# Where ScalarE's read-outs of dense sums and the tanh stand between the exponentials of an attention block with an MLP beside it

## The chip, the cores and the metric

The kernel runs on one core of a Trainium2 chip. The metric is the device time of one execution in microseconds (us), lower is better. Three engines carry the work: TensorE (PE) multiplies, VectorE (DVE) takes row maxima, ScalarE (ACT) takes exponentials; GpSimd (POOL) does elementwise work on the side, and the DMA queue of SyncE (SP) moves data.

## The reference: what is computed

```python
xn = _layernorm(x, axis=-1)                        # x: 2048 x 512
qkv = (xn @ wqkv) ...                              # 32 heads of 16
p = _softmax(q k^T * 16 ** -0.5)                   # 2048 x 2048 for each head
A = (p v) @ wo
h = _gelu(xn @ w1 + b1)                            # 2048 x 1792, tanh form
B = h @ w2 + b2
return x + A + B
```

## The kernel before: how the work is tiled and ordered

**Units and halves.** The attention is cut into tasks of 4 heads by 512 queries, and each task into 16 units; there are 512 units, and `unit` (L633) writes out one of them. A unit has two halves. A half first issues a burst on TensorE: a block of scores S for a later unit, a block of transposed scores T, again an S and a T (`s_half` L245, `e_half` L291). VectorE reduces each S to row maxima (L257). ScalarE turns each T into exponentials `pe` (L302). Behind the burst come, side by side in the two row halves of the array, the products of exponentials and values into `pV` (`v_half` L305) and some *dense* products into `pD` (`dense` L575). A matmul of 64 rows uses one row half, so S beside T and V beside D run at once. V and the dense products change row halves by turns: in the first half of a unit (a = 0, called a B half below) V has rows 64 to 127 and the dense products rows 0 to 63; in the second (a = 1, an A half) it is the other way round. So the order is B, A, B, A and so on.

**Dense groups.** The dense work is everything else: projections of q and k (24 groups), the hidden layer of the MLP (56 groups, `hidden` L1042), its second matrix (16 groups, `store` L1066), the output projection (`finish` L1098). A `Group` (L411) is a list of products that sum into one bank of PSUM. A half issues `pace` products of one row half: FAST is 4, SLOW is 3, and MEAN alternates. Hidden groups alternate SLOW and FAST and so last 8 and 6 halves. A group's last product falls in an A half; the next group starts in the B half that follows.

**Read-outs.** When a group is complete, `ended` (L560) calls `end` (L444): ScalarE reads the sum out of PSUM (`pf` L502, `hh` L1045, `yt` L1068, `ys` L1109), and the bank goes back on a list. `unit` calls `ended` at the end of each half, so the read-out is issued ahead of the next burst's exponentials. `v_end` (L318) reads out `pV` in the same place at the end of each task (`osb` L328, always in a B half).

**GELU.** After `hh` a timed queue (`later` L211, `tick` L233, once a unit) hands out the GELU: three steps on POOL, then the tanh on ScalarE (`t` L1014), then four steps on POOL. `tick` stands behind `ended`, at the end of an A half: a tanh that falls due where a group ends is issued straight behind the read-out.

**Banks.** PSUM has eight banks in lists (L102): S and V share four, T and D the other four. `e_half` takes the bank at the head of list T and puts it at the tail. A dense group takes one bank off the head of the list with its first product (`hold` L112) and puts it at the tail in `end`. So three banks turn among the T blocks while a group holds the fourth, and a T block can start when the reader of its bank is done.

The order on each engine is as written; nothing is rescheduled.

Of the kernel before, what the change touches and what calls it, by code (L numbers as in the profile page):

```python
# [47 lines left out]
def layer_kernel(ctx: ExitStack, tc: tile.TileContext, x, wqkv, wo, w1, b1, w2, b2, out):  # L48
# [110 lines left out]
    def given(engine, ns):  # L159
        backlog[engine] += ns  # L160
# [17 lines left out]
    def leave(user, goes_on):  # L178

        p = newest.pop(user, None)  # L180
        if p is not None and goes_on:
            p.then_inc(turns, 1)
            tc.no_tile_sem_insts.add(p.ins.name)
            counted[0] += 1
            left.append(p)

    def enter():

        if left:
            goal[0] = f"turn{counted[0]}"  # L190
            for p in left:
                tc.add_to_no_dep_group(goal[0], p.ins)
            left.clear()
# [9 lines left out]
    def fetch_scale(m):  # L203

        scale_of[m] = nc.scalar.alloc_register(f"sexp{m}")
        nc.scalar.reg_load(scale_of[m], sexp[0:1, m:m + 1].bitcast(I32))

    mt_of, ptiles, pv_of, stores = {}, {}, {}, {}
    queue, slot = [], [0]

    def later(n, fn, local=False):  # L211
        queue.append((slot[0] + n, fn, local))

    def run_due():
        due = sorted((q for q in queue if q[0] <= slot[0]), key=lambda q: q[0])
        queue[:] = [q for q in queue if q[0] > slot[0]]
        for q in due:
            q[1]()


    steps, room = [], [0]

    def pooled(*todo):
        steps.extend(todo)

    def run_steps(all_of_them=False):
        room[0] = min(room[0], 0) + POOL_NS
        while steps and (room[0] > 0 or all_of_them):
            ns, fn = steps.pop(0)
            room[0] -= ns  # L230
            fn()

    def tick():  # L233
        run_due()
        run_steps()
        slot[0] += 1

    def flush():

        while steps or any(q[2] for q in queue):  # L240
            run_due()
            run_steps(True)
            slot[0] += 1

    def s_half(u, n):  # L245

        t, i = divmod(u, 16)
        g, qb = divmod(t, NQB)
        qt, kb = divmod(i, 4) if t else (i % 4, i // 4)
        if t not in mt_of:  # L250
            mt_of[t] = work.tile([P, 4, 4, 4], F32, name="mt", bufs=2)
        ks, qs = kst[g % 2], qst[g % 2]
        p, a = divmod(n, 2)
        r = slice(64 * a, 64 * a + 62)
        s = banks("S")
        tiled(None, s, qs[p][qb][r, qt * P:(qt + 1) * P], ks[p][kb][r, :], True, True)
        nc.vector.reduce_max(mt_of[t][:, n, qt, kb:kb + 1], s, axis=AX.X)  # L257
        given("dve", 600)
# [32 lines left out]
    def e_half(u, n):  # L291

        p, a = divmod(n, 2)
        t, kt = divmod(u, 16)
        g, qb = divmod(t, NQB)
        st = banks("T")
        r = slice(64 * a, 64 * a + 64)
        k0 = (kt % 4) * P
        tiled(None, st, kst[g % 2][p][kt // 4][r, k0:k0 + P], qst[g % 2][p][qb][r, :], True, True)
        pe = work.tile([P, QB], F32, name="pe", bufs=12)  # L300
        ptiles[u, n] = pe
        nc.scalar.activation(pe, st, AF.Exp, scale=scale_of[g // 2])  # L302
        given("act", 520)

    def v_half(u, a):  # L305

        t, kt = divmod(u, 16)
        g, qb = divmod(t, NQB)
        if kt == 0 and a == 0:
            pv_of[t] = hold("V", "S")  # L310
        pv = pv_of[t][0]
        r = slice(64 * a, 64 * a + 64)
        for h in (2, 3, 0, 1):
            c = (4 * g + h) * VW
            product("V", pv[32 * h:32 * h + 32, :], vv[r, kt, c:c + 32], ptiles[u, h][r],
                    start=(kt == 0 and a == 0), stop=(kt == 15 and a == 1))
# [240 lines left out]
                cur[0], spent[0] = None, True  # L557
        return cur[0]

    def ended():  # L560

        if cur[0] is not None and cur[0].over():
            done, cur[0] = cur[0], None
            done.end()

    def burst(gen, n):

        while n > 0 and (f := group(gen)) is not None:
            if not f.usable():
                break  # L570
            f.product(2)
            n -= 1
            ended()

    def dense(gen, side):  # L575

        f = group(gen)
        for _ in range(0 if f is None else f.pace[pos[0] % 2]):
            if not f.usable(side):
                return  # L580
            f.product(side)
# [25 lines left out]
    def spare(gen, side):  # L607

        if extra[0] is None and not spent[0]:
            f = next(gen, 0)  # L610
            spent[0] = f == 0
            extra[0] = Halves(f) if f else None
        if extra[0] is not None:
            extra[0].product(side)
            if extra[0].at == extra[0].n:
                extra[0] = None

    def land():

        while extra[0] is not None:  # L620
            for side in range(2):
                if extra[0] is not None:
                    spare(None, side)
        if cur[0] is not None:
            enter()
        for side in range(2):
            while cur[0] is not None and cur[0].left(side):
                nc.tensor.drain()
                while cur[0].left(side):
                    cur[0].product(side)  # L630
        ended()

    def unit(gen):  # L633


        u = pos[0]
        e = u - LEAD
        if e >= 0 and e % (2 * NQB * 16) == 0 and e < NU:
            fetch_scale(e // (2 * NQB * 16))
        if u == LEAD and cur[0] is not None:  # L640
            burst(gen, cur[0].left())
        pos[0] += 1
        for a in range(2):
            for b in range(2 * a, 2 * a + 2):
                if u < NU:
                    s_half(u, b)
                elif u > NU:
                    spare(gen, b % 2)
                if 0 <= e < NU:
                    e_half(e, b ^ 1)  # L650
            if u < LEAD:
                burst(gen, LFILL[u - 16] // 2)
            if e >= 0:
                enter()

                w, r = (e - 2, 1) if a == 0 else (e - 1, 0)
                live = 0 <= w < NU
                new = r == 0 and w % 16 == 0
                if live and not new:
                    v_half(w, r)  # L660
                dense(gen, 1 - r)
                if live and new:
                    v_half(w, r)

                for user, goes_on in (("V", live and not (r == 1 and w % 16 == 15)),
                                      ("D", cur[0] is not None and not cur[0].over())):
                    leave(user, goes_on)
                for k in backlog:
                    backlog[k] = max(0, backlog[k] - HALF)
                if live and r == 1:  # L670
                    v_end(w)
                ended()

            if a == 0 and u % 16 == 0 and u // 16 - 1 in stores:
                stores.pop(u // 16 - 1)()
        if u < NU:
            s_end(u)
        tick()
# [325 lines left out]
    def mlp():  # L1004
# [3 lines left out]
        done = set()  # L1008

        def gelu(hh, g, b, f):  # L1010
            t1 = m2.tile([P, QB], F32, name="t1", bufs=2)

            def tanh():
                nc.scalar.activation(t1, t1, AF.Tanh, scale=GELU_C * GELU_A)  # L1014
                given("act", 600)
                later(1, rest, True)

            def rest():
                pooled((690, lambda: nc.gpsimd.tensor_scalar(t1, t1, 1.0, gs[:, 1:2], op0=ALU.add, op1=ALU.mult)),
                       (1280, lambda: nc.gpsimd.tensor_tensor(t1, t1, hh, op=ALU.mult)),  # L1020
                       (620, lambda: nc.gpsimd.tensor_scalar(g[:, 0, f, :], t1, 1.0, 0.0, op0=ALU.mult, op1=ALU.add)),
                       (1160, lambda: nc.gpsimd.tensor_tensor(g[:, 1, f, :], t1, g[:, 0, f, :], op=ALU.subtract)),  # L1022
                       (0, lambda: done.add((b, f))))

            pooled((1040, lambda: nc.gpsimd.tensor_tensor(t1, hh, hh, op=ALU.mult)),  # L1025
                   (620, lambda: nc.gpsimd.tensor_scalar(t1, t1, 1.0, 1.0 / GELU_A, op0=ALU.mult, op1=ALU.add)),
                   (1280, lambda: nc.gpsimd.tensor_tensor(t1, t1, hh, op=ALU.mult)),  # L1027
                   (0, lambda: later(2, tanh, True)))

        for b in range(NQB):  # L1030
            xb = xbs[b]
# [114 lines left out]
    with ExitStack() as st3:  # L1146
# [46 lines left out]
        while pos[0] < NU + LEAD + 2:  # L1193
            more_stacks()
            unit(fil)
# [32 lines left out]
```

## Time and profile before

| what | us |
|---|---|
| median of 3 runs (1520.38 to 1526.5) | 1525.09 |
| the profiled execution, its own time | 1520.55 |
| its span in the trace | 1518.8 |
| TensorE busy | 1489.5 |
| VectorE busy | 1402.2 |
| ScalarE busy | 1245.6 |
| GpSimd busy | 664.5 |

The span begins with the first instruction and ends with the last; 1.75 us of the execution lie around it. A group of instructions is shown as line, engine, operation, output<-inputs, shapes, count, then busy time and mean duration, then the idle time ahead of it and what ended it. Ends of matmuls are modelled, so a busy TensorE says little about whether it could do more. A view of the instructions in order of time merges neighbours of one kind ("x4"), its first column is the start, its second the length.

### The profile page before, as it was taken

The page shows a single profiled execution, that of the slowest core. Times are in us where ns is not written, and L with a number is a line of the kernel's source. Part 1 is how long each engine was busy: PE and PEld are TensorE (multiplying, and loading weights), DVE is VectorE, ACT ScalarE, POOL GpSimd, SP SyncE. Part 2 cuts the span into 40 slices and gives each one's busy share as a digit, 9 for nine tenths or more (in the row PEclk, how much of TensorE's full clock was granted, in tenths as well). Part 3 has the DMA queues.
Part 4 walks back from the last instruction along what each step waited for, and adds up shares of the span by engine and source line. Part 5 has one row for each costly group of instructions (what it writes and reads, how often), then busy time and mean ns, then how long its engine had stood idle before and what let it go on. Part 6 is the DMA issues. An engine that isn't in the chain of part 4 may idle for free.

```text
span 1518.8 us, 86848 instructions
## 1 busy us (share of the span) xinstructions
PE 1489.5 (98%) x39407; PEld 815.9 (54%) x39407; DVE 1402.2 (92%) x2367; ACT 1245.6 (82%) x2318; POOL 664.5 (44%) x686
## 2 busy tenths in 40 slices
PE   8999999999999999999999999999999999999998
PEld 3434555555555555555555555555555555555553
DVE  7899989999999999999999999999999999999933
ACT  5327778899988888898888898988888898888884
POOL 4113597547771112777411167751116775211110
PEclk9999999999999999999999999999999999999998
DMA  6454567542122201121011211122101201121422
GB/s 208 127 155 158 166 219 211 180 126 77 58 69 66 61 26 42 36 84 50 23 49 41 66 42 40 36 78 63 34 25 56 77 27 29 50 60 50 136 65 95
DMA packets 113674, 123.76 MB, mean 81 GB/s; under 512 B 24988, under 2 KB 85276, under 8 KB 113304
## 3 DMA queue, kind: packets, MB, share of 16 engines
q1 hardware_dynamic: 113304, 118.21, 25.4%
q8 instruction: 308, 5.05, 1.4%
q14 instruction: 62, 0.51, 0.1%
HBM read 80.61 MB, written 37.34 MB: 78 GB/s over the span
## 4 chain that ended last, share of the span: by engine, by line
PE 79%; DVE 16%; issue 2%; ACT 2%; DMA 1%; POOL 0%; SPq 0%; POOLq 0%
PE pV L169 23%; PE pD L169 19%; PE pT L169 17%; PE pS L169 16%; DVE mt L257 13%; PE pT L435 1%; PE pD L435 1%; DVE amx L709 1%; ACT pe L302 1%; ACT t L1014 1%; PE pT L528 1%; PE pV L528 0%; DMA m_d<-mhl 0%; DMA xs<-in_A_x_dram 0%; DMA wch<-in_B_w_dram 0%
## 5 line engine op out<-in xcount | busy, mean ns | idle before, releaser
L257 DVE TENSOR_REDUCE mt<-pS 128x1 f32<-128x512 f32 x2048 | 1304.5, 684 | 52.5 <-PE pS L169 34.8
L302 ACT ACTIVATE pe<-pT 128x512 f32<-128x512 f32 x2048 | 1100.8, 599 | 162.9 <-PE pS L169 78.6
L169 PE MATMUL pV<-pe,vv 64*32 64x512 f32 x8192 | 1076.3, 595 | 0.1
L169 PE MATMUL pT<-qst,kst 64*32 64x512 f16 x8192 | 718.3, 378 | 8.8 <-ACT pe L302 7.9
L169 PE MATMUL pS<-kst,qst 62*32 62x512 f16 x8192 | 624.3, 378 | 5.2 <-DVE mt L257 3.6
L169 PEld LDWEIGHTS <-kst 64*32 64x32 f16 x8192 | 285.7, 91 | 203.9 <-issue 103.6
L169 PEld LDWEIGHTS <-qst 62*32 62x32 f16 x8192 | 273.3, 92 | 206.3 <-issue 58.2
L169 PE MATMUL pD<-w_s,g 64*32 64x512 f16 x5376 | 364.6, 376 | 0.0
L169 PE MATMUL pD<-xb,wc 64*32 64x512 f16 x5376 | 360.9, 377 | 0.0
L169 PEld LDWEIGHTS pV<-pe,vv 64*32 64x32 f32 x8192 | 181.0, 105 | 88.3 <-PE pV L169 4.3
L1070 POOL TENSOR_TENSOR xa<-xa,yt 128x512 f32<-128x512 f32 x16 | 20.5, 1282 | 319.0 <-ACT yt L1068 319.0
L169 PEld LDWEIGHTS <-wc 64*32 64x32 f16 x5376 | 116.9, 91 | 41.6
L169 PEld LDWEIGHTS <-g 64*32 64x32 f16 x5376 | 112.2, 91 | 45.3
L169 PE MATMUL pD<-xt,wqk_h 64*32 64x512 f16 x2016 | 134.7, 377 | 1.7 <-issue 1.5
L1025 POOL TENSOR_TENSOR t<-hh 128x512 f32<-128x512 f32 x56 | 58.3, 1041 | 132.7 <-ACT hh L1045 121.8
L358 POOL TENSOR_TENSOR osb<-osb,rb 128x512 f32<-128x512 f32 x31 | 39.9, 1287 | 135.1 <-DMA rb<-den_d 76.0
L1027 POOL TENSOR_TENSOR t<-t,hh 128x512 f32<-128x512 f32 x56 | 71.9, 1284 | 4.7
L1020 POOL TENSOR_TENSOR t<-t,hh 128x512 f32<-128x512 f32 x56 | 71.8, 1281 | 4.7
L1022 POOL TENSOR_TENSOR g<-t,g 128x512 f16<-128x512 f32 x56 | 65.2, 1165 | 4.7
L169 PEld LDWEIGHTS <-wqk_h 64*32 64x32 f16 x2016 | 47.5, 92 | 23.4 <-issue 6.2
L169 PE MATMUL pD<-wo_s,oc 64*32 64x512 f16 x828 | 54.5, 378 | 0.0
L1045 ACT ACTIVATE hh<-pD,b_s,fac 128x512 f32<-128x512 f32 x56 | 43.6, 779 | 9.4 <-PE pT L169 3.3
(141 smaller groups left out, 862.4 us busy)
## 6 DMA issues: line engine op xcount, KB each, us to landing
wch<-in_B_w_dram SPq DMA_DIRECT2D x28, 512.0 KB
wc<-w_d SPq DMA_DIRECT2D x56, 256.0 KB
qk_d<-stg SPq DMA_DIRECT2D x32, 256.0 KB
rb<-den_d SPq DMA_DIRECT2D x124, 64.0 KB
w_d<-wsp SPq DMA_DIRECT2D x28, 256.0 KB
kst<-qk_d SPq DMA_DIRECT2D x128, 48.0 KB
qst<-qk_d SPq DMA_DIRECT2D x128, 48.0 KB
xs<-in_A_x_dram SPq DMA_DIRECT2D x16, 256.0 KB
```

The lines of the kernel that those rows point to most:

```text
L169: p = nc.tensor.matmul(*args, **kw)
L257: nc.vector.reduce_max(mt_of[t][:, n, qt, kb:kb + 1], s, axis=AX.X)
L302: nc.scalar.activation(pe, st, AF.Exp, scale=scale_of[g // 2])
L358: pooled((1280, lambda: nc.gpsimd.tensor_tensor(osb, osb, rb, op=ALU.mult)), (620, lambda: nc.gpsimd.tensor_scalar(ot[:, 0], osb, 1.0, 0.0 ...
L435: nc.tensor.matmul(self.bank, lhs, rhs, start=start, stop=self.last and self.over())
L528: nc.tensor.matmul(pj, xt[:, i, c, t * P:(t + 1) * P], wh[j][:, c, :], start=(n == 0), stop=(n == 11))
L1020: (1280, lambda: nc.gpsimd.tensor_tensor(t1, t1, hh, op=ALU.mult)),
L1022: (1160, lambda: nc.gpsimd.tensor_tensor(g[:, 1, f, :], t1, g[:, 0, f, :], op=ALU.subtract)),
L1025: pooled((1040, lambda: nc.gpsimd.tensor_tensor(t1, hh, hh, op=ALU.mult)), (620, lambda: nc.gpsimd.tensor_scalar(t1, t1, 1.0, 1.0 / GELU_A ...
L1027: (1280, lambda: nc.gpsimd.tensor_tensor(t1, t1, hh, op=ALU.mult)),
L1045: nc.scalar.activation(hh, hp, AF.Identity, scale=scale, bias=bias)
L1070: add = lambda: nc.gpsimd.tensor_tensor(xa, xa, yt, op=ALU.add)
```

## The change

The end of a dense group is no longer carried out where the group's last product is issued. It is put on a list `ends`, and the next half takes it from there: `one_more` stands behind the burst of S and T (and so behind the two exponentials of that burst on ScalarE) and ahead of the half's dense products. It takes one entry: an ended group first, and otherwise one from the list `extras`, into which the GELU now puts its tanh when it falls due. So in the units with exponentials, a half issues at most one of these two kinds. With the read-out, the bank's return to list T moves too: behind the two T blocks of the B half, and ahead of the new group's first product. `osb` stays where it was. In the bursts ahead of the first exponentials, and where a stage ends (`land`, `flush`), ends are carried out at once.

```diff
     def flush():
-        while steps or any(q[2] for q in queue):
+        settle()
+        while steps or extras or any(q[2] for q in queue):
             run_due()
+            while extras:
+                extras.pop(0)()
             run_steps(True)
...
-    def ended():
+    ends, extras = [], []
+
+    def ended(at_once=True):
         if cur[0] is not None and cur[0].over():
             done, cur[0] = cur[0], None
-            done.end()
+            ends.append(done.end)
+            if at_once:
+                settle()
+
+    def settle():
+        while ends:
+            ends.pop(0)()
+
+    def one_more():
+        if ends:
+            ends.pop(0)()
+        elif extras:
+            extras.pop(0)()
...
     def land():
+        settle()
...
             if e >= 0:
+                one_more()
                 enter()
...
                 if live and r == 1:
                     v_end(w)
-                ended()
+                ended(False)
...
-                   (0, lambda: later(2, tanh, True)))
+                   (0, lambda: later(2, lambda: extras.append(tanh), True)))
```

## The prediction

> **What bounds the kernel now.** I read the groups first, then stages, then the order of time.
>
> ```profile
> L257 DVE TENSOR_REDUCE mt<-pS 128x1 f32<-128x512 f32 x2048 | 1304.5, 684 | 52.5 <-PE pS L169 34.8
> L302 ACT ACTIVATE pe<-pT 128x512 f32<-128x512 f32 x2048 | 1100.8, 599 | 162.9 <-PE pS L169 78.6 <-PE pT L169 57.3
> ```
>
> VectorE is nearly full. Its 2048 reductions fill 1304.5 us, 2.55 us for the four of a unit, and were idle for only 52.5 us. ScalarE has slack: 162.9 us ahead of its exponentials. Two stages, second matrix of the MLP and hidden layer, by windows:
>
> ```profile
> 500.00:600.00 100.00, 99.51 (x2792) 56.66 (x2791) 98.71 (x167) 86.26 (x160) 18.38 (x17) 1.00 0.13 37
> 600.00:700.00 100.00, 98.40 (x2776) 54.60 (x2768) 94.57 (x155) 90.08 (x170) 73.00 (x76) 1.00 0.21 60
> ```
>
> The third busy figure is VectorE: 98.7 of 100 us (TensorE, the first, is at 99.5) where ScalarE has hardly anything but exponentials, 94.6 where the hidden layer adds read-outs and tanh. So these do cost time, though ScalarE is not full. How much, and through what, shows in ScalarE's order of time. First quiet stretches, pace SLOW and FAST:
>
> ```profile
> 800.44 2.27 ACT L302 ACTIVATE pe<-pT 128x512 f32<-128x512 f32 x4 [0.28 <-PE pS L169]
> 801.63 1.08 ACT L302 ACTIVATE pe<-pT 128x512 f32<-128x512 f32 x2
> 802.99 2.28 ACT L302 ACTIVATE pe<-pT 128x512 f32<-128x512 f32 x4 [0.28 <-PE pS L169]
> ...
> 282.28 1.08 ACT L302 ACTIVATE pe<-pT 128x512 f32<-128x512 f32 x2 [0.27 <-PE pT L169]
> 283.52 1.09 ACT L302 ACTIVATE pe<-pT 128x512 f32<-128x512 f32 x2 [0.16 <-PE pS L169]
> 284.91 1.09 ACT L302 ACTIVATE pe<-pT 128x512 f32<-128x512 f32 x2 [0.30 <-PE pT L169]
> ```
>
> At SLOW a unit takes 802.99 - 800.44 = 2.55 us (B half 1.19, A half 1.36, the row at 801.63 being the A half); at FAST 284.91 - 282.28 = 2.63 (1.24 and 1.39). Now a hidden group that ends alone, then one that ends with a tanh behind it:
>
> ```profile
> 957.37 1.08 ACT L302 ACTIVATE pe<-pT 128x512 f32<-128x512 f32 x2 [0.30 <-PE pT L169]
> 958.62 1.08 ACT L302 ACTIVATE pe<-pT 128x512 f32<-128x512 f32 x2 [0.16 <-PE pS L169]
> 959.89 0.78 ACT L1045 ACTIVATE hh<-pD,b_s,fac 128x512 f32<-128x512 f32 x1 [0.19 <-PE pT L169]
> 960.57 2.05 ACT L302 ACTIVATE pe<-pT 128x512 f32<-128x512 f32 x4
> 962.47 0.66 ACT L1014 ACTIVATE t<-t 128x512 f32<-128x512 f32 x1
> 962.99 2.16 ACT L302 ACTIVATE pe<-pT 128x512 f32<-128x512 f32 x4
> 965.43 2.28 ACT L302 ACTIVATE pe<-pT 128x512 f32<-128x512 f32 x4 [0.28 <-PE pS L169]
> 967.98 2.27 ACT L302 ACTIVATE pe<-pT 128x512 f32<-128x512 f32 x4 [0.28 <-PE pS L169]
> 970.39 0.78 ACT L1045 ACTIVATE hh<-pD,b_s,fac 128x512 f32<-128x512 f32 x1
> 971.07 0.62 ACT L1014 ACTIVATE t<-t 128x512 f32<-128x512 f32 x1
> 971.59 2.05 ACT L302 ACTIVATE pe<-pT 128x512 f32<-128x512 f32 x4
> 973.91 0.60 ACT L302 ACTIVATE pe<-pT 128x512 f32<-128x512 f32 x1 [0.27 <-PE pT L169]
> ```
>
> Between quiet B halves at 957.37 and 965.43 lie one FAST and two SLOW units, 2.63 + 5.11 = 7.74 us by the quiet rows; they took 8.06. The lone `hh` cost **0.32 us**, the tanh at 962.47 included. From 965.43 to 973.91 lie the same three units: 8.48, so `hh` with the tanh on its heels cost **0.74**. The cost is not the duration (0.78, and 0.78 + 0.62) but a part of it. What is late is the first exponential of the next B half. Its natural distance from the A half before is 1.36 (SLOW) or 1.39 (FAST). Behind `hh` alone it was 960.57 - 958.62 = 1.95, a lag of 0.56; behind the pair 971.59 - 969.17 = 2.42 (the A half in the row of 967.98 begins 1.19 in), a lag of 1.06. Shorter read-outs:
>
> ```profile
> 286.16 1.08 ACT L302 ACTIVATE pe<-pT 128x512 f32<-128x512 f32 x2 [0.16 <-PE pS L169]
> 287.92 2.06 ACT L302 ACTIVATE pe<-pT 128x512 f32<-128x512 f32 x4
> 290.24 0.60 ACT L302 ACTIVATE pe<-pT 128x512 f32<-128x512 f32 x1 [0.26 <-PE pT L169]
> ...
> 790.09 2.28 ACT L302 ACTIVATE pe<-pT 128x512 f32<-128x512 f32 x4 [0.28 <-PE pS L169]
> 793.03 2.05 ACT L302 ACTIVATE pe<-pT 128x512 f32<-128x512 f32 x4
> 795.31 1.81 ACT L302 ACTIVATE pe<-pT 128x512 f32<-128x512 f32 x3 [0.24 <-PE pS L169]
> ```
>
> `pf`: lag 1.76 - 1.39 = 0.37; two FAST units took 290.24 - 284.91 = 5.33 instead of 5.26, a loss of 0.07. `yt`: the A half begins at 791.28, lag 1.75 - 1.36 = 0.39; two SLOW units took 5.22 instead of 5.11, loss 0.11. In all four, **loss = lag less a slack of 0.24 to 0.32**: 0.24 and 0.28 where the next group is SLOW, 0.30 and 0.32 where it is FAST; I use 0.26 and 0.31.
>
> The slack belongs to one wait:
>
> ```profile
> 933.99 0.40 PE L169 MATMUL pT<-qst,kst 64*32 64x512 f16 x4 [0.39 <-ACT pe L302]
> 934.20 0.61 PE L169 MATMUL pV<-pe,vv 64*32 64x512 f32 x4
> ```
>
> With three T banks, the second T block of an A half takes the bank that the first T block of the B half before it had, and must wait for that first exponential. These are TensorE's rows behind another pair of `hh` and tanh: the second T is released by an exponential, and V, in the same row half and behind it in TensorE's order, starts 0.21 later. The view of waits lists only 20 such stalls:
>
> ```profile
> PE pT L169 <- ACT pe L302: 7.9, 20, 0.7
> ```
>
> 7.9 us is too low, as modelled matmul ends cover part of each gap; the 34.8 us that VectorE's reductions waited for S blocks (their row above) are the same loss seen from the engine that it starves.
>
> **The change part by part.** No instruction is added or removed. TensorE's order stays as it is, since the change moves only ends and the tanh; the steps on POOL and the stores on SP that follow come one to three halves later. POOL is busy 73% even in the hidden stage's row above, and SP's stores have whole units to land, so I cost these at nothing; without that cover a later tanh would hold up the second matrix's first group, whose last hidden tile is wanted only 13 units after it starts.
>
> *The tanh leaves the read-out.* The pairs stand 18 times in the trace, first and last at
>
> ```profile
> 335.40 0.62 ACT L1014 ACTIVATE t<-t 128x512 f32<-128x512 f32 x1
> ...
> 1231.71 0.62 ACT L1014 ACTIVATE t<-t 128x512 f32<-128x512 f32 x1
> ```
>
> Alone it costs nothing: at 962.47 it follows an A half's exponentials at once (they begin 2.05 - 1.08 = 0.97 into the row of 960.57, at 961.54), and the next come 1.45 later, a lag of 0.09, inside the slack. I take zero before and after.
>
> *The read-out moves behind the B half's exponentials.* It no longer waits for the group's last product (the 0.19 idle ahead of `hh`). The B exponentials run on time. Those of the next A half are late: the read-out starts 0.97 after the first B exponential, as that tanh did, and holds ScalarE for 960.57 - 959.89 = 0.68, against a B half of 1.19 to 1.24, a lag of 0.41 to 0.46. Who waits for that is the second T of the following B half, and its burst is itself put off by 0.17 to 0.22 through the next step; what is left of the lag, 0.24, is within the slack. I take zero.
>
> *The bank comes back later: the wait that replaces the old one.* Follow list T. Before: p, q, r, A half takes p and q, then r, p, q, and the end adds D. B takes r and p, the new group q; the next A half takes D and **r**, whose exponential was B's first. After: B takes r and p, then D is added, the new group takes q; the next A half takes r and **p**, and p was B's *second* T. So its second T now waits for B's second exponential, which ends 1.08 - 0.60 = 0.48 us after the first (two take 1.08, one 0.60 by its group's mean). That acts as a lag of 0.48 at the same wait, with the same slack: it costs 0.48 - 0.31 = 0.17 where the next group is FAST, 0.22 where it is SLOW, whichever read-out it is. Queued behind that T on TensorE are V, the dense products and the next burst, so VectorE starves as before. Bounds: zero, if the slack were wholly another's; 0.48, if there were none. I take the middle value since it lies between two measured lags, 0.37 and 0.56.
>
> The sum, with counts from these rows and the 56 hidden groups:
>
> ```profile
> L1045 ACT ACTIVATE hh<-pD,b_s,fac 128x512 f32<-128x512 f32 x56 | 43.6, 779 | 9.4 <-PE pT L169 3.3 <-PE pS L169 2.8
> L502 ACT ACTIVATE pf<-pD 128x512 f32<-128x512 f32 x22 | 13.1, 597 | 7.4 <-PE pD L435 2.9 <-PE pS L169 2.3 <-PE pT L169 2.2
> L1068 ACT ACTIVATE yt<-pD,gs 128x512 f32<-128x512 f32 x16 | 11.0, 688 | 1.5 <-PE pT L169 0.2
> L1109 ACT ACTIVATE ys<-pD,gs 128x512 f32<-128x512 f32 x8 | 5.5, 687 | 1.0 <-PE pT L169 0.6
> ```
>
> - 18 `hh` with tanh, next FAST: 0.74 to 0.17, -10.3 us
> - 10 `hh` alone, next FAST: 0.56 - 0.31 = 0.25 to 0.17, -0.8
> - 28 `hh`, next SLOW: 0.56 - 0.26 = 0.30 to 0.22, -2.2
> - 22 `pf`, next FAST: 0.07 to 0.17, +2.2
> - 16 `yt`, next taken as SLOW: 0.11 to 0.22, +1.8
> - 8 `ys`, next FAST: taken at 0.06, near `pf`, to 0.17, +0.9
>
> Losses fall from 28.0 to 19.6: **-8.4 us**. Some read-outs meet an `osb` in both kernels, which I take as even. The profiled execution's 1520.55 becomes 1512.1, or -0.55%; on the median of 1525.09, 0.3% above that execution, the same share gives **1516.7 us**.
>
> The Trainium skill, page "Perfetto Trace Analysis", section "Optimization Strategy", says that the same gap coming back on the engine that should be full can mean that no PSUM was left for the next tile. By that rule a bank held half a unit longer is a loss in itself; the trace agrees at 933.99, and at the full 0.48 the sum would be a loss, the second rival below.
>
> **The rivals.** *The bank wait is hidden.* If A's second T has other cover, only the gain is left, up to -28.0: 1497 on the median, 1505 if each read-out still costs 0.08. For it: ScalarE would no longer be late where it matters. Against it: the losses above follow this very wait. *The bank wait is dearer*, the slower case: the second T waits for ScalarE in person, so any lateness of the B exponentials (an `osb` or a tanh shortly before) adds to it without slack. There are 102 read-outs, so it decides at 28.0 / 102 = 0.27 us each; at 0.35 the change is +7.7, 1533, at the full 0.48 +21, 1546. For it: 0.27 is near my 0.17 to 0.22. Against it: a B half's exponentials lie a whole half after any tanh. *The tanh stays in the way*: were it due in the half of each read-out, pairs would form again and the time stay at 1525; the rule of one a half excludes it, save beside `osb`.
>
> **How the numbers follow.** Forecast (-4 to -13 us) 0.62, hidden 0.16, dearer 0.20, tanh in the way 0.02. About 0.5%, 7.6 us, is what a measurement here can tell from no change; the forecast lies near that line, so its 0.62 splits into 0.33 faster and 0.29 within, and 0.06 of the dearer case stays within: faster 0.33 + 0.16 = 0.49, same 0.29 + 0.06 + 0.02 = 0.37, slower 0.14. Range 1504 (hidden, nearly) to 1532 (dearer at 0.34).
>
> **What would show it.** No `t` straight behind `hh`. The stretch with the pair costs 0.17 over its quiet units instead of 0.74, the one with `hh` alone 0.22 instead of 0.32. The second T of the A half after a read-out starts just as B's second exponential ends, V 0.2 late. VectorE's wait on S falls by some 8 us; around `pf` and `yt` it grows. If those units run at 2.55 and 2.63 undisturbed, the first rival is right; if each read-out costs over 0.3, the second.

## The result, and the profile after

The kernel changed takes **1514.65 us** (median of 7 runs, 1513.3 to 1516.93) against 1525.09 for the kernel before (also 7 runs, 1518.94 to 1527.1): ratio **0.9945**, 95% interval 0.9927 to 0.9962. The prediction said 1516.7 and 0.55% less. The profiled execution took 1513.79, its span is 1512.0. Lines have moved: L257 is L260 now, L302 is L305, L1045 is L1065.

The same groups and waits of the changed kernel as were shown of before (the last two are the view of waits: us in total, times, longest):

```profile
L260 DVE TENSOR_REDUCE mt<-pS 128x1 f32<-128x512 f32 x2048 | 1304.7, 684 | 41.8 <-PE pS L169 25.9
L305 ACT ACTIVATE pe<-pT 128x512 f32<-128x512 f32 x2048 | 1112.3, 598 | 172.4 <-PE pS L169 82.0
L1065 ACT ACTIVATE hh<-pD,b_s,fac 128x512 f32<-128x512 f32 x56 | 43.9, 783 | 0.0
...
PE pT L169 <- ACT pe L305: 1.2, 2, 1.0
DVE mt L260 <- PE pS L169: 25.9, 89, 1.4
```

VectorE's reductions are as busy as before (1304.7 us against 1304.5); their idle time fell from 52.5 to 41.8, and of this the wait for S blocks from 34.8 to 25.9. Of these 8.9 us, 8.5 lie after 320 us (23.2 to 14.7 there), behind the projections; the span of the profiled execution lost 6.8. `hh` had 9.4 us of idle time ahead of it and has none. TensorE's visible stalls behind exponentials fell from 20 to 2. Of the 20, 17 stood behind pairs of `hh` and tanh and all of these went; the other three, and the two that are left, lie in the first 190 us. In the trace after, no tanh stands straight behind a read-out.

By stages (columns as before, VectorE the third busy figure):

```profile
500.00:600.00 100.00, 99.50 (x2804) 56.71 (x2791) 98.61 (x166) 86.20 (x160) 17.73 (x17) 1.00 0.13 37
600.00:700.00 100.00, 99.96 (x2838) 56.60 (x2836) 96.73 (x158) 91.98 (x173) 72.73 (x77) 1.00 0.22 61
```

The hidden layer's stretch went from 94.57 to 96.73; the second matrix's lost a little, 98.71 to 98.61. ScalarE's order of time, first a read-out followed by a SLOW group, then one followed by a FAST group:

```profile
918.45 1.08 ACT L305 ACTIVATE pe<-pT 128x512 f32<-128x512 f32 x2 [0.30 <-PE pT L169]
919.43 0.78 ACT L1065 ACTIVATE hh<-pD,b_s,fac 128x512 f32<-128x512 f32 x1
920.09 3.45 ACT L305 ACTIVATE pe<-pT 128x512 f32<-128x512 f32 x6
923.81 1.08 ACT L305 ACTIVATE pe<-pT 128x512 f32<-128x512 f32 x2 [0.28 <-PE pS L169]
...
966.54 1.08 ACT L305 ACTIVATE pe<-pT 128x512 f32<-128x512 f32 x2 [0.28 <-PE pS L169]
967.52 0.78 ACT L1065 ACTIVATE hh<-pD,b_s,fac 128x512 f32<-128x512 f32 x1
970.33 0.63 ACT L1034 ACTIVATE t<-t 128x512 f32<-128x512 f32 x1
974.63 0.60 ACT L305 ACTIVATE pe<-pT 128x512 f32<-128x512 f32 x1 [0.30 <-PE pT L169]
```

From 918.45 to 923.81 lie two SLOW units, 5.11 us when quiet; they took 5.36, a loss of **0.25** (forecast 0.22; before, 0.32). From 966.54 to 974.63 lie three FAST units, 7.90 when quiet; they took 8.09, a loss of **0.19** (forecast 0.17; before, 0.74 with the tanh on its heels). The tanh, three halves behind the group's end at 970.33, adds nothing. And the wait that was to take the old one's place, on TensorE behind the read-out at 967.52, with VectorE's answer:

```profile
967.68 0.40 PE L169 MATMUL pT<-qst,kst 64*32 64x512 f16 x4
967.89 0.61 PE L169 MATMUL pV<-pe,vv 64*32 64x512 f32 x4
...
969.24 1.29 DVE L260 TENSOR_REDUCE mt<-pS 128x1 f32<-128x512 f32 x2 [0.23 <-PE pS L169]
```

The B half's two exponentials run from 966.54 to 967.62; the second T starts 0.06 later, V 0.21 behind it, and VectorE then stands idle for 0.23. The wait is there though the view of waits no longer lists it.

The same can be read for every read-out. All kernels here issue the same 512 units of exponentials, so each unit of one trace has its counterpart in another. Below, a *frame* is three units: from the first exponential of the B half one unit ahead of a read-out's old place to the first exponential of the B half three units later. Its length in one trace less its length in the trace of before is what a kernel gains or loses at that read-out.

### The profile page after: what moved, and what is told of

The parts are those of the page before. It is cut to its first block, busy times and chain, and to the rows that moved or that the text cites. A ratio compares the mean times of both kernels' runs of the same rounds, so it can differ in the third digit from the quotient of the medians.

```text
span 1512.0 us, 86779 instructions
## 1 busy us (share of the span) xinstructions
PE 1489.9 (99%) x39407; PEld 822.7 (54%) x39407; DVE 1405.0 (93%) x2368; ACT 1244.0 (82%) x2317; POOL 663.7 (44%) x685
## 3 DMA queue, kind: packets, MB, share of 16 engines
q1 hardware_dynamic: 113304, 118.21, 25.9%
## 4 chain that ended last, share of the span: by engine, by line
PE 81%; DVE 16%; issue 1%; DMA 1%; ACT 1%; POOL 0%; SPq 0%; ACTq 0%; POOLq 0%
PE pV L169 24%; PE pD L169 20%; PE pT L169 17%; PE pS L169 17%; DVE mt L260 14%; PE pT L438 1%; PE pD L438 1%; DVE amx L729 1%; PE pT L531 1%; PE pV L531 0%; DMA wq<-in_A_wqkv_dram 0%; DMA wch<-in_B_w_dram 0%; PE pT L799 0%; PE pS L438 0%; POOL xt L804 0%
## 5 line engine op out<-in xcount | busy, mean ns | idle before, releaser
L260 DVE TENSOR_REDUCE mt<-pS 128x1 f32<-128x512 f32 x2048 | 1304.7, 684 | 41.8 <-PE pS L169 25.9
L305 ACT ACTIVATE pe<-pT 128x512 f32<-128x512 f32 x2048 | 1112.3, 598 | 172.4 <-PE pS L169 82.0
L169 PEld LDWEIGHTS <-kst 64*32 64x32 f16 x8192 | 289.4, 91 | 191.8 <-issue 94.2
L1045 POOL TENSOR_TENSOR t<-hh 128x512 f32<-128x512 f32 x56 | 58.3, 1041 | 86.5 <-ACT hh L1065 85.4
L1039 POOL TENSOR_SCALAR t<-t,gs 128x512 f32<-128x512 f32 x56 | 39.0, 696 | 49.7 <-ACT t L1034 49.3
```

The costliest lines, as they stand in the source:

```text
L169: p = nc.tensor.matmul(*args, **kw)
```

## The experiments

The theory of the prediction is that a read-out costs what the A half's second T waits beyond its slack: for the B half's first exponential, put off by the read-out, or, with the bank given back late, for its second. Rivals: the read-out's own place is what counts; or ScalarE's lateness counts whoever waits, and the banks don't matter. The first four ran against before at 1523.69 us, the last three against 1522.68. Edits are shown against the changed kernel, and the last run makes its edit in the kernel before.

**The tanh alone.**

```diff
-                ended(False)
+                ended()
```

> Only the tanh goes through the list; the end of a group stays where it was. Theory of the prediction (a read-out costs its lag less a slack at the A half's second T, and a late bank costs as much as a lag of 0.48): the 18 pairs become lone read-outs, 0.74 to 0.25 us each, and nothing else changes: -8.8 us, ratio 0.994, as much as the whole change. Rival (what pays is that the read-out leaves the way of the next exponentials): the read-outs still stand there, so about 1.000, at most 0.998.

Measured: 1514.49 us, ratio 0.9942 (0.9929 to 0.9954). The whole gain is there with every read-out in its old place. ScalarE's order where a pair stood before:

```profile
964.21 2.28 ACT L305 ACTIVATE pe<-pT 128x512 f32<-128x512 f32 x4 [0.28 <-PE pS L169]
966.62 0.78 ACT L1065 ACTIVATE hh<-pD,b_s,fac 128x512 f32<-128x512 f32 x1
967.30 1.08 ACT L305 ACTIVATE pe<-pT 128x512 f32<-128x512 f32 x2
968.26 0.64 ACT L1034 ACTIVATE t<-t 128x512 f32<-128x512 f32 x1
972.42 0.60 ACT L305 ACTIVATE pe<-pT 128x512 f32<-128x512 f32 x1 [0.31 <-PE pT L169]
```

From 964.21 to 972.42 lie one SLOW and two FAST units, 7.82 when quiet; they took 8.21. The loss is 0.39, not the 0.25 expected. The tanh now stands one half behind the read-out, between the exponentials of the B and the A half; that it finds some of the read-out's lag there is likely and was not tested. 18 times 0.74 - 0.39 is 6.3 us, and the spans of the two profiled executions differ by 6.6 (1518.8 and 1512.2). The medians differ by 9.2, with an interval from 7 to 11; where the rest would lie, no trace tells.

**The read-outs alone.**

```diff
-                   (0, lambda: later(2, lambda: extras.append(tanh), True)))
+                   (0, lambda: later(2, tanh, True)))
```

> Only the ends of groups go behind the next burst; the tanh is issued as it falls due. Theory of the prediction: losses as in the whole change (19.6 us against 28.0), but 18 tanh now stand ahead of the B half's exponentials in which a read-out follows, and pass their lag of 0.09 on to the late bank: about -6.8 us, ratio 0.9955. Rival (the read-out leaving the way pays, the tanh matters little): the same 0.9945 as the whole change. Were the tanh the whole of it, 1.000 or above.

Measured: 1517.12 us, ratio 0.9952 (0.9938 to 0.9966), near the 0.9955 expected; the rival's 0.9945 lies in the interval too, so the time alone doesn't decide. The traces do: the 18 frames with a pair lose 6.6 us with the tanh alone, 8.7 with the read-outs alone and 9.8 with both. Each part alone gives most of it, since either one takes the pairs apart. That the read-out leaves the way of the next exponentials is thus not needed for the gain.

**The bank alone, late.** ScalarE's order is that of before; only the return to list T waits for the next half. (`give_back` is the return, the last two lines of `end`, made a method of its own.)

```diff
-            ends.append(done.end)
+            done.finish(done.bank)
+            ends.append(done.give_back)
...
-                   (0, lambda: later(2, lambda: extras.append(tanh), True)))
+                   (0, lambda: later(2, tanh, True)))
```

> ScalarE's order as before the change, but the bank of an ended group goes back on its list only behind the next burst. Theory of the prediction (the late bank makes the A half's second T wait for the B half's second exponential, 0.48 us after the first): the lag of every read-out grows by 0.48 at that wait, so the losses rise from 28 to about 77 us: +49 us, ratio 1.032. Rival (what is left of the loss is ScalarE's lateness itself, whoever waits for it, and the banks don't matter): 1.000.

Measured: 1563.81 us (2 runs, 1563.11 and 1564.51), ratio 1.0261 (1.0243 to 1.0279), 40 us slower: with no instruction moved on ScalarE, the bank by itself costs more than anything else in this study. ScalarE and TensorE around a pair, and the waits:

```profile
954.65 2.28 ACT L305 ACTIVATE pe<-pT 128x512 f32<-128x512 f32 x4 [0.28 <-PE pS L169]
959.62 0.78 ACT L1069 ACTIVATE hh<-pD,b_s,fac 128x512 f32<-128x512 f32 x1
960.82 2.17 ACT L305 ACTIVATE pe<-pT 128x512 f32<-128x512 f32 x4
963.62 0.60 ACT L305 ACTIVATE pe<-pT 128x512 f32<-128x512 f32 x1 [0.64 <-PE pT L169]
...
961.45 0.40 PE L169 MATMUL pT<-qst,kst 64*32 64x512 f16 x4 [0.58 <-ACT pe L305]
961.94 0.40 PE L169 MATMUL pT<-qst,kst 64*32 64x512 f16 x4
962.15 0.61 PE L169 MATMUL pV<-pe,vv 64*32 64x512 f32 x4
...
DVE mt L260 <- PE pS L169: 74.2, 130, 1.8
```

From 954.65 to 963.62, two SLOW units and a FAST one, 8.97 us; the same stretch took 8.48 in the kernel before. The difference, **0.49**, is the distance between the two exponentials. Both T blocks of the A half are now seen to wait, the first for the B half's first exponential (961.45), the second for its second (961.94). VectorE waits 74.2 us for S instead of 34.8: 39.4 more, of the 43.9 by which the spans of the two profiled executions differ (1562.7 and 1518.8). The expected 49 took 0.48 for every one of 102 read-outs; the 40 between the medians is 0.39 on average. By the frames, `hh`, `yt` and `ys` each cost 0.49 more in the median, as foreseen, and `pf` only 0.33, for a reason that no run here shows; all frames together cost 44.0. Here the rule of the Trainium skill that the prediction weighed (page "Perfetto Trace Analysis", section "Optimization Strategy", a gap that keeps coming back can mean that no PSUM was left) is borne out by a number.

**Only the hidden layer's read-outs late.**

```diff
-            if at_once:
+            if at_once or not done.late:
...
-                             for c in range(NC) for i, j in PAIRS], dbank, hidden, pace=FAST if f % 2 else SLOW)
+                             for c in range(NC) for i, j in PAIRS], dbank, hidden, pace=FAST if f % 2 else SLOW, late=True)
```

(`late` is a new mark of a `Group`, False unless given.)

> The whole change, but only the hidden layer's read-outs go behind the next burst; those of the projections, of the second matrix and of the output projection stay at the end of the half. Theory of the prediction: these three pay less at once (0.06 to 0.11 us) than the late bank costs them (0.17 to 0.22): losses 28 x 0.17 + 28 x 0.22 + 3.8 = 14.8 us against 28.0 before, -13.2 us, ratio 0.991. Rival (a read-out behind the burst is never worse): 0.9945 or above.

Measured: 1512.29 us, ratio 0.9923 (0.9908 to 0.9939). Its expected 0.991 lies inside; the interval overlaps the whole change's, so that it is better than the whole change is likely and not shown. The traces show it for one kind: the 16 frames with a `yt` are 0.09 us longer than before with the whole change (median) and 0.00 here.

**T ahead of S in the B half**, an attempt to bring the B half's exponentials, and with them the bank, forward. First with the whole change:

```diff
             for b in range(2 * a, 2 * a + 2):
+                if a == 0 and b == 0 and 0 <= e < NU:
+                    e_half(e, 1)
                 if u < NU:
                     s_half(u, b)
...
-                if 0 <= e < NU:
+                if b and 0 <= e < NU:
                     e_half(e, b ^ 1)
```

> The whole change, and in the B half the first T block is written ahead of the first S block. In a quiet SLOW unit of before, T's row half was free at 802.23 and S's at 802.42, but the exponential started at 802.99, 0.57 after S, since S stands first. Theory of the prediction: at SLOW the B half's exponentials come about 0.2 earlier, the late bank with them, and the 0.22 of each read-out that is followed by a SLOW group (44 of 102) goes; at FAST both row halves come free together and nothing changes. Losses 9.9 us against 28.0 before: -18 us, ratio 0.988. Rival (the exponential waits for something else, or S behind T starves VectorE): 0.9945 or above.

Measured: 1508.74 us, ratio 0.9906 (0.9887 to 0.9925): faster than the change alone, by 5.9 us between the medians (the intervals don't touch, by a hair) where 9.7 were expected; the expected 0.988 lies just outside the interval. The same with only the hidden layer's read-outs late:

> Only the hidden layer's read-outs and the tanh go behind the burst, and T stands first in the B half. Theory: losses 28 x 0.17 + about 2 for the projections' and the output's read-outs = 7 us against 28.0: -21 us, ratio 0.986, the least of all. Rival as for T first: 0.992 or above, as without it.

Measured: 1508.55 us, ratio 0.9903 (0.9885 to 0.9922), the lowest median of the study, but not to be told from the 1508.74 just before. Its interval and that of the whole change don't touch. The expected 0.986 lies outside: this expectation failed too. It counted on T first and on sparing `yt` and the others the late bank, as two gains; but with T first and the whole change, the late bank no longer costs a `yt` anything (its frame is 0.01 shorter than before, in the median), so there was little left to spare. And T first with nothing of the change:

> The kernel before with T first in the B half and nothing of the change. Theory: the slack at the A half's second T grows by about 0.2 to 0.26 where the group that follows is SLOW, so 28 lone hidden read-outs fall from 0.30 to about 0.05 us and 16 of the second matrix from 0.11 to 0; the 18 pairs, followed by FAST groups, keep their 0.74: -9 us, ratio 0.994. Rival (S behind T starves VectorE): 1.000 or above.

Measured: 1523.08 us, ratio 1.0001 (0.9988 to 1.0014). The expectation failed. Two views say why; quiet halves of this kernel at SLOW and a pair:

```profile
967.32 1.09 ACT L302 ACTIVATE pe<-pT 128x512 f32<-128x512 f32 x2 [0.18 <-PE pT L169]
968.61 1.09 ACT L302 ACTIVATE pe<-pT 128x512 f32<-128x512 f32 x2 [0.20 <-PE pS L169]
969.88 1.08 ACT L302 ACTIVATE pe<-pT 128x512 f32<-128x512 f32 x2 [0.18 <-PE pT L169]
971.10 0.78 ACT L1047 ACTIVATE hh<-pD,b_s,fac 128x512 f32<-128x512 f32 x1
971.78 0.62 ACT L1016 ACTIVATE t<-t 128x512 f32<-128x512 f32 x1
972.30 0.58 ACT L302 ACTIVATE pe<-pT 128x512 f32<-128x512 f32 x1
```

A quiet B half follows its A half by 968.61 - 967.32 = 1.29 instead of 1.36: T first brings its exponential forward by 0.07 to 0.08, not by the 0.2 expected. And behind the pair it comes 972.30 - 969.88 = 2.42 after the A half, exactly as before: it starts when the read-out and the tanh are done, however early T is. So with the read-out ahead of the exponentials T first is worth nothing, and with the read-out behind them it can move the late bank by the whole 0.07. The trace of the whole change with T first shows the latter:

```profile
919.14 1.09 ACT L305 ACTIVATE pe<-pT 128x512 f32<-128x512 f32 x2 [0.24 <-PE pT L169]
920.11 0.78 ACT L1067 ACTIVATE hh<-pD,b_s,fac 128x512 f32<-128x512 f32 x1
924.42 1.09 ACT L305 ACTIVATE pe<-pT 128x512 f32<-128x512 f32 x2 [0.20 <-PE pS L169]
```

Two SLOW units from 919.14 to 924.42, 5.28 us: 0.08 less than the 5.36 of the whole change at 918.45. At 0.06 to 0.08 for each of the 102 read-outs that is 6 to 8 us; the medians differ by 5.9. The expectation had the gain at SLOW alone. By the frames it comes at FAST as well: against the whole change, T first takes 0.06 us off the frame of a pair and 0.08 off that of a lone `hh` before a FAST group, 0.08 before a SLOW group and 0.10 off that of a `yt` (medians). Why at FAST too was not looked into.

## Why the prediction was right

By kind of read-out, the forecast and the frames of the trace after against those of before (21 of the 22 `pf` stand among the units):

| read-outs | each, forecast | each, median | together, forecast | together |
|---|---|---|---|---|
| 18 `hh` with tanh | -0.57 | -0.56 | -10.3 | -9.8 |
| 10 `hh` alone, next FAST | -0.08 | +0.02 | -0.8 | +0.2 |
| 28 `hh`, next SLOW | -0.08 | -0.06 | -2.2 | -1.4 |
| 21 `pf` | +0.10 | 0.00 | +2.2 | -1.1 |
| 16 `yt` | +0.11 | +0.09 | +1.8 | +1.2 |
| 8 `ys` | +0.11 | 0.00 | +0.9 | +1.0 |

Together they lose 10.0 us where 8.4 were forecast; the units outside the frames take 2.1 longer, 1.5 of it in the first two units. The mechanism and the one large term came out. That the ratio is the forecast one almost to the digit is luck: the smaller terms are off by up to their own size and more, and the differences partly cancel.

- **What bounds the kernel.** VectorE is starved by the A half's T blocks, which wait for their banks. The late bank alone, which changes nothing but the banks that these T blocks get, moved VectorE's wait for S by 39.4 us and the span by 43.9. Shown. But the 34.8 us of before are not all this loss, as the prediction had it: 11.5 of them lie before 320 us and hardly changed (11.1 after).
- **Loss is lag less slack.** It gave 0.17 and 0.22 for the late bank; the two events shown above have 0.19 and 0.25. The wait ends 0.06 after the second exponential, as foreseen.
- **The tanh leaves the read-out.** No pair is left and the stalls behind them are gone; the term of -10.3 us is -9.8. That the tanh alone gains as much time as the whole change agrees, with the reservation above.
- **Lone hidden read-outs.** The term of -2.2 is -1.4. The term of -0.8 has not come: before a FAST group a lone `hh` costs as much as it did. Why is open.
- **`pf`, `yt`, `ys` pay for the late bank.** For `yt` this is so. For `pf` it is not shown: its frames differ by anything from -1.10 to +0.76, and scatter as widely where its read-out was left in place (-0.93 to +0.99 with only the hidden read-outs late), and the median is 0.00 in both. The eight `ys` scatter too. Leaving all three where they were is worth 2.4 us between the medians of two series (1514.65 and 1512.29), where their +4.9 together were forecast. One `pf` and one `yt` in the trace after:

```profile
288.84 1.08 ACT L305 ACTIVATE pe<-pT 128x512 f32<-128x512 f32 x2 [0.28 <-PE pT L169]
294.29 0.60 ACT L305 ACTIVATE pe<-pT 128x512 f32<-128x512 f32 x1 [0.30 <-PE pT L169]
...
789.48 1.08 ACT L305 ACTIVATE pe<-pT 128x512 f32<-128x512 f32 x2 [0.28 <-PE pS L169]
794.83 1.08 ACT L305 ACTIVATE pe<-pT 128x512 f32<-128x512 f32 x2 [0.28 <-PE pS L169]
```

Two FAST units with a `pf` at 288.84 take 5.45 instead of 5.33 (forecast +0.10), two SLOW units with a `yt` at 789.48 take 5.35 instead of 5.22 (forecast +0.11). The `yt` is typical of its kind, the `pf` is not.

- **The rivals.** The bank wait is neither hidden nor dearer, and the tanh is out of the way. With the read-out ahead of the exponentials the same late bank costs 0.49 each (the bank alone, late): there the slack is already used up. What "hidden" would be worth is bounded by nothing that ran; T first took some 6 us of it.
- **The chances.** The ratio lies on the 0.5% that a measurement can tell from no change, where the forecast had been put.

## What to carry to other kernels

When a read-out is moved, follow the bank that it frees: the return to the list is a wait of its own, and here it was worth more than the read-out's place (+40 us by itself). Where small operations on an idle-looking engine cost time, price them as lag less slack at the wait that they delay, from two or three events of different length, and look for two of them in a row before moving each one: taking pairs apart was nearly the whole gain here. A part of a gain that another part gives as well isn't to be added up.

## What the runs showed of the hardware

- In a SLOW unit's B half, a T block in the row half that came free first started ahead of an S block that is written before it. In the kernel before, with S first in the B half, and in the one with T first:

```profile
802.23 0.39 PE L169 MATMUL pT<-qst,kst 64*32 64x512 f16 x4
802.42 0.42 PE L169 MATMUL pS<-kst,qst 62*32 62x512 f16 x8
```

```profile
787.49 0.39 PE L169 MATMUL pT<-qst,kst 64*32 64x512 f16 x4
787.67 0.42 PE L169 MATMUL pS<-kst,qst 62*32 62x512 f16 x8
...
788.17 0.60 ACT L302 ACTIVATE pe<-pT 128x512 f32<-128x512 f32 x1 [0.20 <-PE pS L169]
```

  By the kernel, the first S of the half has rows 0 to 61 and this T rows 64 to 127. T starts 0.19 us ahead of S although S is written first, and writing T first leaves that at 0.18, which fits that T first brought so little. The exponential starts 0.76 after T with S first (802.99) and 0.68 with T first, against 0.49 in an A half (T at 801.14, exponential at 801.63). So 0.08 of the 0.27 us between 0.76 and 0.49 belongs to the order, and what the other 0.19 is made of stays open. The Trainium skill, page "TensorE: Matmul & The Clock Gate", section "The mechanism", says that matmuls keep program order in start and end. The starts of this trace don't, across row halves; of the ends the trace can't tell, since they are modelled.
- TensorE's view of waits listed 20 stalls of 7.9 us in all before and 2 of 1.2 after; VectorE's waits for S were 34.8 us and 25.9. The waits of some 0.2 us that the late bank leaves, as at 967.68, are in no row of TensorE's view and show only on the engine that is starved. But VectorE's sum compares kernels of one order alone: with T first in the kernel before it is 43.3 us instead of 34.8, at the same time (1523.08 us and 1522.68).
